# One DMA transpose per 256-token unit for the queries and one for the keys, with other step orders

## The chip, the cores and the metric

The kernel runs on one core of one Trainium2 chip. The metric is device time in microseconds of one execution, as a median over runs. The kernel before took 244.47 us (two runs, 244.05 and 244.89).

## The reference

Retention with a decay per head, then a feed-forward layer with a SoLU activation and a layer norm. Batch 8, 8 heads, 576 positions, head width 64; 4608 tokens, model width 512, hidden width 1024.

```python
scores = scale * np.matmul(q, k.transpose(0, 1, 3, 2))
gamma = 1.0 - 2.0 ** (-5.0 - np.arange(H))
Dmat = np.where(rel >= 0, gamma[:, None, None] ** rel[None, :, :], 0.0)   # rel = row - column
x = np.matmul(scores * Dmat[None], v)          # then tokens x 512
h = x @ w_in
e = np.exp(h - h_max); sm = e / (np.sum(e, axis=-1, keepdims=True) + 1e-09)
solu = h * sm
ln = (solu - mu) / np.sqrt(var + 1e-06) * g_ln
out = ln @ w_out
```

## The kernel before

The 4608 tokens are cut into 36 chunks of up to 128 tokens. For two batch entries at a time there are nine: four **units** of 256 tokens (two chunks each, numbered 0-1, 2-3, 4-5, 6-7) and a ninth chunk, 8, that holds the last 64 positions of both entries. Chunks 9 to 17 are the next nine, and so on to 35. A unit is loaded with one DMA of 512 KB for each of q, k and v; the ninth chunk with two of 128 KB each.

The work is a list of small steps, written out by hand as text: START, then LOOP twice (chunk numbers moved by 9 and 18), then END (numbers counted back from 35). A token such as `cq:10:v` is step `cq` for chunk 10 on VectorE (`a` ScalarE, `v` VectorE, `g` GpSimd). Each engine executes its own instructions strictly in the order of this list, and so does SyncE (SP), which issues nearly all DMAs: an instruction that waits holds everything behind it on its engine.

The steps, with their lines in the kernel before:

- `ld` (L204, L206) loads q, k or v; `lo` (L699) a quarter of w_out; `li` (L694, on GpSimd's queue) a quarter of w_in. The loads of q, k, v and w_out share 14 buffers, which go round.
- `cq`, `cv` (L228) scale q and v and cast them to 16 bits, `ck` (L194) casts k. Before, each chunk has its own buffer (q16: 5 of them, k16: 6).
- The scores need q and k transposed, in a tile qkT for each unit (3 buffers). For chunks 0 to 5 and every ninth chunk TensorE does it (`tr`, L251) and `er` (L194) copies the result out of PSUM. For all others a DMA transpose from SBUF to SBUF does it: `kd` (L259) for the keys, `kq` (L266) for the queries, one for each chunk, 52 in all. In START, `kq` and `kd` of chunks 0 to 5 do nothing.
- `sc` (L293, L299) scores, `mk` (L312) masks them, `kv` (L327) is k times v for the running state, `ad`, `d3`, `dk` (L342, L344, L368, L356) carry the state on, `av` (L385) and `fs` (L406) make the chunk's output, `ex` (L194) copies it to xT.
- `m1` (L443) is the first feed-forward matmul (eight of 128x512), `mx` (L453) its row maximum, `xp` (L459) the exponential, `so` (L468) the product, `ce` (L479, L484) a centring that only chunks 0 to 4 have, `sq` and `rt` (L494, L496, L508 to L518) the norm, `tu` (L526) and `eu` (L194) a transposition, `m2` (L541) the second matmul, `st` (L549, L554) the scaling and the store.
- `wo` (L706) casts an eighth of w_out, `mm`, `mc`, `ws` (L723, L194, L732) make its centred copy. The first five `m2` need all eight `wo`.
- `wu` (L671) issues so many matmuls of zeros whose result nothing reads: 33 in all, in START.
- The last chunk's feed-forward part is cut in halves: `hm`, `hx`, `hp`, `ho`, `ht`, `he`, `hq`, `h2`, `hw` (L564 to L664).

BANKS gives, in the order of the list, the PSUM bank (0 to 3) of each small PSUM tile.

START of before begins as below; `v` of the first unit comes after four loads of q, three of k and one quarter of w_out.

```
ld:0:k c1:0 wu:0:7 ld:0:q wu:0:1 ld:2:q ld:2:k ld:4:q ck:0:g cq:3:g ck:3:a cq:1:v ck:1:g
cq:5:v kq:2 cq:2:g cq:0:g lo:1 li:2 ld:4:k tr:1 ck:2:a tr:3 ld:0:v ...
```

Of the kernel before, what the change touches and what calls it, by code (L numbers as in the profile page):

```python
# [31 lines left out]
fs:2 cq:7:g ex:2:a ad:3 d3:3 mx:0 lo:2 cq:6:g fs:3 mk:5 sc:4 lo:0 xp:0 so:0 ck:6:g ex:3:a
ld:13:q mx:1 xp:1 mk:4 wo:4:a cv:6:g dk:3 kv:4 wo:5:a m1:3 ad:4 kd:6 wo:0:a kq:7 av:4 kq:6
cv:8:g so:1 ce:0 fs:4 ck:7:g mx:3 dk:4 m1:2 fs:5 sq:0 ce:1 kd:7 xp:3 d3:4 mx:2 ex:4:a ex:5:a
lo:3 ad:5 xp:2 cq:14:g cq:13:g wu:0:9 so:3 cv:7:g sc:6 sc:7 ld:9:k m1:4 mk:7 kv:6 mk:6 tu:1
wo:1:a ld:8:q ad:6 wo:6:a rt:0 so:2 ld:9:v ce:3 wo:7:a d3:6 ld:8:k tu:0 dk:6 mx:4 mm:0 ck:9:g
m1:5 ce:2 ck:10:a eu:1:a ad:7 ld:9:q mc:0:a sq:1 dk:5 kd:0 eu:0:v cq:8:g av:6 fs:6 fs:7 xp:4
# [22 lines left out]
st:5 kd:11 mx:8 eu:6:a sc:10 tu:7 sq:7 rt:7 ld:18:q m2:6 kv:9 mk:10 kd:13 eu:7:a m2:7 ld:13:v  # L60
kq:14 ad:9 cv:12:g d3:9 xp:8 so:8 av:9 ad:10 dk:9 fs:10 fs:9 tu:8 sc:12 st:6 ex:9:v m1:9
ld:18:k eu:8:v mk:12 kv:11 st:7 kq:13 sc:11 ex:10:a sq:8 mx:9 ad:11 m1:10 mk:11 cq:16:g rt:8
ck:16:g xp:9 so:9 cq:18:g m2:8 dk:11 av:11 fs:12 kd:14 ld:20:k d3:11 ad:12 fs:11 tu:9 mx:10
eu:9:v ex:11:a m1:11 sc:13 cv:13:g xp:10 cq:15:g ld:15:v m2:9 kd:16 ex:12:a
# [2 lines left out]
kq:-1 sc:-3 cv:-3:g d3:-7 sq:-8 dk:-7 kv:-4 ld:0:v so:-7 ld:0:k mk:-4 m1:-5 ld:0:q st:-9 rt:-8
cq:0:g st:-8 mx:-6 xp:-6 ad:-4 d3:-4 mk:-3 kq:-2 av:-4 dk:-4 so:-6 ck:-2:a sq:-7 fs:-3 ad:-3
mx:-5 fs:-4 ex:-3:a tu:-6 ck:0:g ex:-4:a kd:-2 sc:-1 tr:0 cv:-1:g cv:-2:g tu:-7 kv:-2 d3:-5
m1:-3 eu:-6:a mk:-1 er:0:v ad:-2 xp:-5 dk:-5 so:-5 sc:-2 mk:-2 mx:-3 rt:-7 cv:0:g eu:-7:a  # L70
m1:-4 av:-2 fs:-2 sq:-5 sq:-6 tu:-5 d3:-2 dk:-2 ad:-1 xp:-3 mx:-4 eu:-5:a m2:-6 ex:-2:a rt:-6
# [41 lines left out]
def kernel(  # L113
# [111 lines left out]

    def scaled(n, key, out, table, engine):
        dst = half.tile([P, H, D], F16, name=out, bufs=5)
        engine.tensor_tensor(  # L228
            out=dst, in0=T.pop((key, n)), in1=table.unsqueeze(2).to_broadcast([P, H, D]),
            op=ALU.mult,  # L230
        )
# [4 lines left out]

    def ck(n, e="g"):
        k16 = half.tile([P, H, D], F16, name="k16", bufs=6)
        copy(ENG[e], k16, T.pop(("kf", n)))
        T["k16", n] = k16  # L240

    def cv(n, e="g"):
        scaled(n, "vf", "v16", gkt if chunks[n][1] == 4 else gk[:, 8 * half_of(n) : 8 * half_of(n) + 8], ENG[e])
# [9 lines left out]
                )  # L253
        T["tp", n] = tp

    def kd(n):
# [2 lines left out]
        nc.sync.dma_start_transpose(  # L259
            out=turned(n)[:, 1, half_of(n)], in_=T["k16", n].rearrange("p h d -> p (h d)")  # L260
        )

    def kq(n):
        if chunks[n][1] == 4 or n < BY_DMA:
            return
        nc.sync.dma_start_transpose(  # L266
            out=turned(n)[:, 0, half_of(n)], in_=T.pop(("q16", n)).rearrange("p h d -> p (h d)")
        )
# [511 lines left out]
```

## Time and profile before

| | |
|---|---|
| median of the runs | 244.47 us |
| profiled execution, its own time | 246.94 us |
| its span, first to last instruction | 245.1 us |
| mean granted TensorE clock | 0.950 |
| matmuls, transposes by TensorE included | 2721, PE busy 211.1 us (86%) |
| VectorE, ScalarE, GpSimd busy | 181.4, 158.1, 161.8 us |
| moved by DMA | 48.42 MB, mean 198 GB/s |

The groups that the steps of this case are priced with, from the profile's list of instruction groups (engine, what, count, mean duration):

| step | engine and shape | count | mean ns |
|---|---|---|---|
| m1 | PE 128x512 | 280 | 394 |
| mk | DVE 128x512 from PSUM | 72 | 683 |
| mx, so | DVE 128x1024 | 35, 35 | 1216, 1217 |
| xp | ACT 128x1024 | 35 | 1115 |
| er, eu | ACT, DVE 128x1024 | | 1012, 681 |
| cq | POOL, DVE 128x512 | 28, 8 | 1062, 731 |
| ck | POOL, ACT 128x512 | 13, 18 | 640, 621 |
| dk, d3 | POOL 128x512, 128x256 | 32, 24 | 1070, 612 |
| kd, kq | SP, issue of one DMA transpose | 26, 26 | medians 1290, 1296 |

A reader may go by the time at which `m1` of a chunk starts, which is found by counting groups of eight L443 matmuls in PE's timeline: the first starts at 33.66 us, the fourth at 43.73, that of chunk 12 at 98.40, chunk 21 at 150.90, chunk 30 at 205.85, chunk 34 at 225.93.

### The profile page before, as it was taken

The numbers are of one execution on the slowest core, as the hardware profiler recorded it, in microseconds if no ns is written. First come the engines' busy times: TensorE is split into PE (matmuls) and PEld (weight loads), VectorE is DVE, ScalarE is ACT, GpSimd is POOL, SyncE is SP. The second block draws the span as 40 slices with busy tenths as digits, with TensorE's granted clock in tenths as the row PEclk, the third lists the DMA queues.
The fourth block names the chain that finished last, engine by engine and source line by source line (L and its number), as shares of the span: only waits on it lengthen the run. The fifth ranks groups of instructions, "written<-read, shape, count | busy, mean of one in ns | idle before, by whom it ended". The sixth has DMA issues, their size and how long they took to land.

```text
span 245.1 us, 6736 instructions
## 1 busy us (share of the span) xinstructions
PE 211.1 (86%) x2721; PEld 114.1 (47%) x2721; DVE 181.4 (74%) x289; ACT 158.1 (64%) x261; POOL 161.8 (66%) x249
## 2 busy tenths in 40 slices
PE   5166499999978999998599999995699999799993
PEld 1052264556534555545345555552345544555551
DVE  0173659999779888995659897991669898799731
ACT  2013036969695376979539548967439458689891
POOL 1393698859499655898716795789617695996121
PEclk9997689999999999999679999999689999999999
DMA  7999998799989999989949999999948998101125
GB/s 188 267 303 236 298 260 146 206 224 219 233 225 233 299 162 270 199 234 235 222 123 215 244 214 214 198 260 197 270 126 201 216 198 192 24 4 43 45 87 173
DMA packets 99456, 48.42 MB, mean 198 GB/s; under 512 B 43872, under 2 KB 93408, under 8 KB 99424
## 3 DMA queue, kind: packets, MB, share of 16 engines
q1 hardware_dynamic: 97216, 46.54, 89.8%
q0 software_dynamic: 576, 1.05, 2.3%
q10 hardware_dynamic: 1632, 0.40, 0.9%
q8 instruction: 21, 0.34, 0.7%
q14 instruction: 11, 0.09, 0.2%
HBM read 32.77 MB, written 9.44 MB: 172 GB/s over the span
## 4 chain that ended last, share of the span: by engine, by line
PE 46%; DMA 18%; DVE 9%; SPq 8%; ACT 7%; POOL 6%; issue 5%; POOLq 0%; DVEq 0%; ACTq 0%
PE o L541 16%; PE h L443 14%; DMA qkT<-q 7%; DMA vf<-in_v_dram 6%; PE lp L526 4%; SPq L204 4%; DMA qf<-in_q_dram 4%; DVE u L468 3%; SPq L206 3%; PE x L385 3%; ACT xT L194 2%; PE sc L293 2%; POOL s L356 2%; ACT e L459 2%; DMA kf<-in_k_dram 2%
## 5 line engine op out<-in xcount | busy, mean ns | idle before, releaser
L443 PE MATMUL h<-w_in,xT 128*128 128x512 f16 x280 | 69.8, 394 | 0.6 <-DVE u L468 0.4
L541 PE MATMUL o<-w_cen,uT 128*128 128x512 f16 x240 | 56.5, 379 | 0.1
L312 DVE TENSOR_TENSOR ret<-sc,tris 128x512 f16<-128x512 f32 x72 | 46.1, 683 | 8.3 <-PE sc L299 6.7
L459 ACT ACTIVATE e<-h,nm 128x1024 f32<-128x1024 f32 x35 | 39.0, 1115 | 12.1 <-DVE nm L453 10.4
L468 DVE SCALAR_TENSOR_TENSOR u<-h,e 128x1024 f16<-128x1024 f32 x35 | 42.5, 1217 | 4.7 <-ACT e L459 4.6
L453 DVE TENSOR_REDUCE nm<-h 128x1 f32<-128x1024 f32 x35 | 42.6, 1216 | 3.6 <-PE h L443 3.6
L443 PEld LDWEIGHTS <-xT 128*128 128x128 f16 x280 | 26.2, 101 | 29.7 <-issue 3.7
L541 PEld LDWEIGHTS <-uT 128*128 128x128 f16 x280 | 25.8, 98 | 29.0 <-issue 2.4
L356 POOL TENSOR_TENSOR s<-t,small 128x512 f16<-128x512 f32 x32 | 34.2, 1070 | 6.3 <-DVE t L344 4.6
L228 POOL TENSOR_TENSOR q<-qf,small 128x512 f16<-128x512 f32 x28 | 29.7, 1062 | 12.9 <-DMA qf<-in_q_dram 9.5
L228 POOL TENSOR_TENSOR v<-vf,small 128x512 f16<-128x512 f32 x29 | 32.0, 1106 | 6.6 <-DMA vf<-in_v_dram 6.5
L496 ACT ACTIVATE sq<-u,su 128x1024 bf16<-128x1024 f16 x30 | 34.5, 1151 | 1.1 <-DVE u L468 1.1
L194 ACT CAST xT<-x 128x512 f16<-128x512 f32 x27 | 19.1, 723 | 22.7 <-PE x L385 15.3
L549 ACT ACTIVATE o_sb<-o,rs 128x512 f32<-128x512 f32 x35 | 23.9, 690 | 14.2 <-issue 7.5
L514 POOL TENSOR_SCALAR w<-ss,w 128x1 f32<-128x1 f32 x31 | 8.2, 265 | 32.1 <-ACT sq L496 30.3
L526 PE MATMUL lp<-ident,u 128*128 128x128 f16 x280 | 22.7, 229 | 7.3 <-DVE t L344 7.0
L526 PEld LDWEIGHTS <-u 128*128 128x128 f16 x280 | 18.7, 102 | 12.8 <-issue 7.6
L194 ACT COPY uT<-lp 128x1024 f16<-128x1024 f16 x17 | 17.2, 1011 | 10.7 <-PE lp L526 10.7
L228 DVE TENSOR_TENSOR q<-qf,small 128x512 f16<-128x512 f32 x8 | 5.9, 731 | 22.4 <-DMA qf<-in_q_dram 12.0
L518 POOL TENSOR_TENSOR rs<-w,mhalf 128x1 f32<-128x1 f32 x36 | 19.8, 549 | 3.0
L293 PE MATMUL sc<-qkT 64*64 64x128 f16 x512 | 14.6, 226 | 7.7 <-DVE ret L312 6.0
L368 POOL TENSOR_TENSOR s<-t,small 128x256 f32<-128x256 f32 x24 | 14.7, 612 | 6.4 <-DVE t L344 4.1
(71 smaller groups left out, 252.3 us busy)
## 6 DMA issues: line engine op xcount, KB each, us to landing
kf<-in_k_dram SPq DMA_DIRECT2D x16, 512.0 KB, 5.8
qf<-in_q_dram SPq DMA_DIRECT2D x16, 512.0 KB, 6.7
vf<-in_v_dram SPq DMA_DIRECT2D x16, 512.0 KB, 6.7
out_dram<-o_sb SPq DMA_DIRECT2D x32, 256.0 KB, 4.7
w_out<-in_moe_w_out_dram SPq DMA_DIRECT2D x4, 512.0 KB, 6.8
w_in<-in_moe_w_in_dram POOLq DMA_DIRECT2D x4, 256.0 KB, 7.2
vf<-in_v_dram SPq DMA_DIRECT2D x8, 128.0 KB, 5.5
qf<-in_q_dram SPq DMA_DIRECT2D x8, 128.0 KB, 4.8
```

The costliest lines, as they stand in the source:

```text
L194: (engine.copy if engine is nc.scalar else engine.tensor_copy)(out=out, in_=in_)
L228: engine.tensor_tensor(out=dst, in0=T.pop((key, n)), in1=table.unsqueeze(2).to_broadcast([P, H, D]), op=ALU.mult,)
L312: nc.vector.tensor_tensor(out=r, in0=s, in1=m, op=ALU.mult)
L356: nc.gpsimd.tensor_tensor(out=s16, in0=t.unsqueeze(2).to_broadcast([P, 4, 2, D]), in1=gd.unsqueeze(3).to_broadcast([P, 4, 2, D]), op=ALU.mult,
L443: nc.tensor.matmul(out=h[:, i * 512 : (i + 1) * 512], lhsT=xT[:, d], rhs=w_in16[:, d, i * 512 : (i + 1) * 512], start=d == 0, stop=d == 3,)
L453: nc.vector.tensor_reduce(out=nm, in_=T["h", n], axis=AX.X, op=ALU.max, negate=True)
L459: nc.scalar.activation(out=e, in_=T["h", n], func=ACT.Exp, bias=T.pop(("nm", n)), accum_out=s)
L468: nc.vector.scalar_tensor_tensor(out=u, in0=T.pop(("h", n)), scalar=-1.0, in1=T.pop(("e", n)), op0=ALU.mult, op1=ALU.mult, accum_out=su,)
L496: nc.scalar.activation(out=s, in_=T.pop(("v", n)), func=ACT.Square, scale=-float(DFF), bias=T.pop(("su", n)), accum_out=ss,)
L526: nc.tensor.transpose(out=lp[:, c], in_=u[:, c * P : (c + 1) * P], identity=ident)
L541: nc.tensor.matmul(out=o, lhsT=uT[:, c], rhs=w[:, c], start=c == 0, stop=c == NF - 1)
L549: nc.scalar.activation(out=o_sb, in_=T.pop(("o", n)), func=ACT.Copy, scale=T.pop(("rs", n)))
```

## The change

A unit's two chunks share one 16-bit buffer for q (3 buffers of a unit) and one for k (4), in place of one buffer for each chunk. One DMA transpose of 128 x 1024 turns a unit's queries and one its keys; 26 DMA transposes in place of 52. Chunks 0 to 5 and the ninth chunks still go through TensorE.

```diff
+    def cast(key, n):
+        if key == "v16":
+            return half.tile([P, H, D], F16, name=key, bufs=5)
+        u = unit(n)
+        if (key, "pair", u) not in T:
+            T[key, "pair", u] = half.tile(
+                [P, 2, H, D], F16, name=key, bufs=3 if key == "q16" else 4
+            )
+        return T[key, "pair", u][:, half_of(n)]
...
-    def kd(n):
+    def turn(n, i, key):
         if chunks[n][1] == 4 or n < BY_DMA:
             return
+        assert (key, n) in T and (key, n + 1) in T
         nc.sync.dma_start_transpose(
-            out=turned(n)[:, 1, half_of(n)], in_=T["k16", n].rearrange("p h d -> p (h d)")
+            out=turned(n)[:, i].rearrange("p t a b -> p (t a) b"),
+            in_=T[key, "pair", unit(n)].rearrange("p t h d -> p (t h d)"),
         )
```

LOOP is the same list but for `kq` and `kd`: sixteen tokens become eight, each right behind the second of the two casts that it reads (`ck:6:a kd:6`, `cq:10:v kq:9`, `ck:10:v kd:9`, `cq:11:v kq:11`, and so on).

START and END are other lists, and BANKS another string. No `wu` is left. The front of START and the back of END:

```diff
-ld:0:k c1:0 wu:0:7 ld:0:q wu:0:1 ld:2:q ld:2:k ld:4:q ck:0:g cq:3:g ck:3:a cq:1:v ck:1:g
...
+c1:0 ld:0:k ld:0:q ld:0:v li:0 li:1 li:2 li:3 c2:0 cq:0:g ld:2:k ld:2:q ld:4:q lo:0 lo:1 lo:2
+lo:3 ld:2:v ck:0:a tr:0 er:0:a ck:3:a cq:1:v kq:0 cq:4:g ld:4:k ck:1:v tr:1 er:1:v kd:0 cq:3:g
+tr:3 er:3:v cq:2:v kq:2 cv:0:g ld:6:k ck:2:v tr:2 er:2:a kd:2 ld:6:q cv:1:g sc:0 ck:4:g tr:4
+er:4:a cq:5:g kq:4 ck:5:a tr:5 er:5:v kd:4 cv:2:v mk:0 sc:1 ld:9:q kv:0 mk:1 ld:4:v ad:0
+cv:3:g d3:0 av:0 ad:1 dk:0 fs:1 fs:0 sc:3 ex:0:v m1:0 ld:9:k mk:3 kv:2 sc:2 ex:1:a mx:0 ad:2
+m1:1 mk:2 cq:7:g ck:7:g xp:0 so:0 ce:0 cq:9:g dk:2 av:2 fs:3 ld:11:k d3:2 ad:3 fs:2 tu:0 mx:1
+eu:0:v ex:2:a m1:2 sc:4 cv:4:g xp:1 cq:6:g kq:6 ld:6:v wo:0:a wo:1:v wo:2:g wo:3:a wo:4:v
+wo:5:g wo:6:a wo:7:v m2:0 ex:3:a ld:11:q d3:1 cv:5:g ck:6:a kd:6 so:1 ce:1 sq:0 tu:1 ld:13:q
+rt:0 mk:4 sc:5 mx:2 eu:1:a m1:3 ...
...
-eu:-4:a hp:0:0 m2:-3 ht:0:1 he:0:1:v m2:-4 ho:0:0 sq:-2 hc:0 rt:-3 st:-3 tu:-2 ht:0:0 rt:-4
-mx:-1 eu:-2:a m2:-7 xp:-1 m2:-5 st:-4 he:0:0:a so:-1 tu:-1 rt:-2 hq:0:0:a st:-7 hq:0:1:a
-eu:-1:v rt:0 m2:-2 h2:0:0 sq:-1 st:-5 st:-2 hw:0:0:v rt:-1 m2:-1 st:-1 h2:0:1 hw:0:1:v
+eu:-4:a sq:-3 dk:-1 m1:-1 cv:0:g sc:0 m2:-4 mx:-2 eu:-3:v mk:0 xp:-2 st:-4 mx:-1 xp:-1 so:-2
+sq:-2 av:0 rt:-3 fs:0 ex:0:v rt:-2 m2:-3 tu:-2 so:-1 st:-3 eu:-2:a tu:-1 sq:-1 rt:-1 m2:-2
+eu:-1:a m2:-1 st:-2 st:-1 hm:0:0 hx:0:0 hm:0:1 hx:0:1 hp:0:0 hp:0:1 ho:0:0 ho:0:1 hc:0 ht:0:0
+he:0:0:v ht:0:1 he:0:1:a hq:0:0:a hq:0:1:a h2:0:0 rt:0 h2:0:1 hw:0:0:a hw:0:1:v
```

SP's first loads are therefore, after: k, q, v of unit 0-1; k, q of unit 2-3; q of 4-5; four quarters of w_out; v of 2-3; k of 4-5; k, q of 6-7.

More of the change, by code (lines that the diff above doesn't have):

```diff
@@ L32 @@
[L32 to L37, printed above, removed]
@@ new lines @@
+wo:5:g wo:6:a wo:7:v m2:0 ex:3:a ld:11:q d3:1 cv:5:g ck:6:a kd:6 so:1 ce:1 sq:0 tu:1 ld:13:q
+rt:0 mk:4 sc:5 mx:2 eu:1:a m1:3 mk:5 kv:4 av:4 st:0 dk:1 ad:4 fs:4 d3:3 ld:8:q xp:2 so:2 ce:2
+m2:1 cv:6:g ld:8:k tu:2 ld:11:v dk:4 mx:3 d3:4 sq:1 ex:4:a ck:9:a ld:9:v fs:5 ck:12:a m1:4
+ad:5 cq:10:v kq:9 sc:6 xp:3 eu:2:v rt:1 ld:8:v st:1 cv:7:g sq:2 so:3 ce:3 mk:6 mx:4 m2:2 tu:3
+ex:5:a eu:3:v sc:7 cq:13:g xp:4 rt:2 mk:7 m1:5 dk:3 cq:8:g ld:13:k ck:10:v kd:9 st:2 kv:6 av:6
+fs:6 ad:6 dk:5 m2:3 mx:5 sq:3 ck:8:a d3:6 so:4 ce:4 ex:6:a dk:6 xp:5 rt:3 cq:12:g cq:11:v
@@ new lines @@
+kq:11 fs:7 tr:8 m1:6 ad:7 so:5 cv:9:g sq:4 er:8:a rt:4 tu:4 tu:5 ex:7:a st:3 ld:15:k ck:11:v
+kd:11 eu:4:a sq:5 dk:7 m1:7 cv:8:g sc:8 mm:0 mc:0:a ws:0:v ws:1:v ws:2:g ws:3:v ws:4:v ws:5:g
+ws:6:v ws:7:v m2:4 mx:6 eu:5:v mk:8 xp:6 st:4 mx:7 xp:7 so:6 sq:6 ld:15:q av:8 cv:10:g sc:9
+rt:5 fs:8 ex:8:v rt:6 ck:13:g cq:14:g kq:13 ck:14:a kd:13 m2:5 tu:6 m1:8 cv:11:v so:7 mk:9
+st:5 mx:8 eu:6:a sc:10 tu:7 sq:7 rt:7 ld:18:q m2:6 kv:9 mk:10 eu:7:a m2:7 ld:13:v ad:9 cv:12:g
+d3:9 xp:8 so:8 av:9 ad:10 dk:9 fs:10 fs:9 tu:8 sc:12 st:6 ex:9:v m1:9 ld:18:k eu:8:v mk:12
@@ L49 @@
+kv:11 st:7 sc:11 ex:10:a sq:8 mx:9 ad:11 m1:10 mk:11 cq:16:g rt:8 ck:16:g xp:9 so:9 cq:18:g
+m2:8 dk:11 av:11 fs:12 ld:20:k d3:11 ad:12 fs:11 tu:9 mx:10 eu:9:v ex:11:a m1:11 sc:13 cv:13:g
+xp:10 cq:15:g kq:15 ld:15:v m2:9 ex:12:a
 """
 LOOP = """
-ld:11:q d3:1 cv:5:g ck:6:a so:1 kq:7 kd:6 kq:6 sq:0 tu:1 ld:13:q rt:0 mk:4 sc:5 mx:2 st:-1
-eu:1:a kv:-55 m1:3 mk:5 kv:4 av:4 st:0 dk:1 ad:4 fs:4 d3:3 ld:8:q xp:2 so:2 m2:1 cv:6:g ld:8:k
-tu:2 ld:11:v dk:4 mx:3 d3:4 sq:1 ex:4:a ck:9:a ld:9:v fs:5 ck:12:a m1:4 ad:5 cq:10:v sc:6 kd:9
@@ L60 @@
[L60 to L64, printed above, removed]
+ld:11:q d3:1 cv:5:g ck:6:a kd:6 so:1 sq:0 tu:1 ld:13:q rt:0 mk:4 sc:5 mx:2 st:-1 eu:1:a kv:-55
@@ new lines @@
+m1:3 mk:5 kv:4 av:4 st:0 dk:1 ad:4 fs:4 d3:3 ld:8:q xp:2 so:2 m2:1 cv:6:g ld:8:k tu:2 ld:11:v
+dk:4 mx:3 d3:4 sq:1 ex:4:a ck:9:a ld:9:v fs:5 ck:12:a m1:4 ad:5 cq:10:v kq:9 sc:6 xp:3 eu:2:v
+rt:1 ld:8:v st:1 cv:7:g sq:2 so:3 mk:6 mx:4 m2:2 tu:3 ex:5:a eu:3:v sc:7 cq:13:g xp:4 rt:2
+mk:7 m1:5 dk:3 cq:8:g ld:13:k ck:10:v kd:9 st:2 kv:6 av:6 fs:6 ad:6 dk:5 m2:3 mx:5 sq:3 ck:8:a
+d3:6 so:4 ex:6:a dk:6 xp:5 rt:3 cq:12:g cq:11:v kq:11 fs:7 tr:8 m1:6 ad:7 so:5 cv:9:g sq:4
+er:8:a rt:4 tu:4 tu:5 ex:7:a st:3 ld:15:k ck:11:v kd:11 eu:4:a sq:5 dk:7 m1:7 cv:8:g sc:8 m2:4
@@ new lines @@
+mx:6 eu:5:v mk:8 xp:6 st:4 mx:7 xp:7 so:6 sq:6 ld:15:q av:8 cv:10:g sc:9 rt:5 fs:8 ex:8:v rt:6
+ck:13:g cq:14:g kq:13 ck:14:a kd:13 m2:5 tu:6 m1:8 cv:11:v so:7 mk:9 st:5 mx:8 eu:6:a sc:10
+tu:7 sq:7 rt:7 ld:18:q m2:6 kv:9 mk:10 eu:7:a m2:7 ld:13:v ad:9 cv:12:g d3:9 xp:8 so:8 av:9
+ad:10 dk:9 fs:10 fs:9 tu:8 sc:12 st:6 ex:9:v m1:9 ld:18:k eu:8:v mk:12 kv:11 st:7 sc:11
+ex:10:a sq:8 mx:9 ad:11 m1:10 mk:11 cq:16:g rt:8 ck:16:g xp:9 so:9 cq:18:g m2:8 dk:11 av:11
+fs:12 ld:20:k d3:11 ad:12 fs:11 tu:9 mx:10 eu:9:v ex:11:a m1:11 sc:13 cv:13:g xp:10 cq:15:g
@@ L65 @@
+kq:15 ld:15:v m2:9 ex:12:a
 """
 END = """
[L67 to L71, printed above, removed]
@@ L72 @@
-fs:-1 xp:-4 dk:-1 dk:-3 so:-3 sc:0 mk:0 so:-4 m1:-2 av:0 sq:-3 fs:0 st:-6 ex:0:a ex:-1:v sq:-4
-tu:-3 tu:-4 mx:-2 hm:0:0 rt:-5 hm:0:1 eu:-3:v hx:0:0 xp:-2 hx:0:1 so:-2 hp:0:1 m1:-1 ho:0:1
-eu:-4:a hp:0:0 m2:-3 ht:0:1 he:0:1:v m2:-4 ho:0:0 sq:-2 hc:0 rt:-3 st:-3 tu:-2 ht:0:0 rt:-4
-mx:-1 eu:-2:a m2:-7 xp:-1 m2:-5 st:-4 he:0:0:a so:-1 tu:-1 rt:-2 hq:0:0:a st:-7 hq:0:1:a
-eu:-1:v rt:0 m2:-2 h2:0:0 sq:-1 st:-5 st:-2 hw:0:0:v rt:-1 m2:-1 st:-1 h2:0:1 hw:0:1:v
+d3:-7 cv:-3:g ck:-2:a kd:-2 so:-7 sq:-8 tu:-7 rt:-8 mk:-4 sc:-3 mx:-6 st:-9 eu:-7:a m1:-5
@@ new lines @@
+mk:-3 kv:-4 av:-4 st:-8 dk:-7 ad:-4 fs:-4 d3:-5 ld:0:q xp:-6 so:-6 m2:-7 cv:-2:g ld:0:k tu:-6
+dk:-4 mx:-5 d3:-4 sq:-7 ex:-4:a fs:-3 m1:-4 ad:-3 sc:-2 xp:-5 eu:-6:v rt:-7 ld:0:v st:-7
+cv:-1:g sq:-6 so:-5 mk:-2 mx:-4 m2:-6 tu:-5 ex:-3:a eu:-5:v sc:-1 xp:-4 rt:-6 mk:-1 m1:-3
+dk:-5 cq:0:g st:-6 kv:-2 av:-2 fs:-2 ad:-2 dk:-3 m2:-5 mx:-3 sq:-5 ck:0:a d3:-2 so:-4 ex:-2:a
+dk:-2 xp:-3 rt:-5 fs:-1 tr:0 m1:-2 ad:-1 so:-3 sq:-4 er:0:a rt:-4 tu:-4 tu:-3 ex:-1:a st:-5
+eu:-4:a sq:-3 dk:-1 m1:-1 cv:0:g sc:0 m2:-4 mx:-2 eu:-3:v mk:0 xp:-2 st:-4 mx:-1 xp:-1 so:-2
@@ L77 @@
+sq:-2 av:0 rt:-3 fs:0 ex:0:v rt:-2 m2:-3 tu:-2 so:-1 st:-3 eu:-2:a tu:-1 sq:-1 rt:-1 m2:-2
+eu:-1:a m2:-1 st:-2 st:-1 hm:0:0 hx:0:0 hm:0:1 hx:0:1 hp:0:0 hp:0:1 ho:0:0 ho:0:1 hc:0 ht:0:0
+he:0:0:v ht:0:1 he:0:1:a hq:0:0:a hq:0:1:a h2:0:0 rt:0 h2:0:1 hw:0:0:a hw:0:1:v
 """
 BANKS = """
-012301321032103032102013123031031203103212103202130230123023021320321302132012003210320301301230
-212013213201232013201323021320312031203103202302120312303201301320313201320131230132103210321021
-323120313201231023013020101230120231203102
+012301232301230123012012310230123021203123120322013220132013201321032103210213231230321031213201
@@ L83 @@
+201321132013201320132012301230123120102103012302120132132012201320132013201321032103210213231230
+32103121320120132101321032103210321
 """
@@ L224, in turned @@
         return T["qkT", u]
+    def cast(key, n):
[7 more added lines that the diff above has]
+        return T[key, "pair", u][:, half_of(n)]
     def scaled(n, key, out, table, engine):
-        dst = half.tile([P, H, D], F16, name=out, bufs=5)
+        dst = cast(out, n)
         engine.tensor_tensor(
@@ L237, in ck @@
     def ck(n, e="g"):
-        k16 = half.tile([P, H, D], F16, name="k16", bufs=6)
+        k16 = cast("k16", n)
         copy(ENG[e], k16, T.pop(("kf", n)))
@@ L254, in tq, with kd @@
         T["tp", n] = tp
-    def kd(n):
+    def turn(n, i, key):
         if chunks[n][1] == 4 or n < BY_DMA:
             return
+        assert (key, n) in T and (key, n + 1) in T
         nc.sync.dma_start_transpose(
-            out=turned(n)[:, 1, half_of(n)], in_=T["k16", n].rearrange("p h d -> p (h d)")
+            out=turned(n)[:, i].rearrange("p t a b -> p (t a) b"),
+            in_=T[key, "pair", unit(n)].rearrange("p t h d -> p (t h d)"),
         )
     def kq(n):
[L264 to L268, printed above, removed]
+        turn(n, 0, "q16")
+    def kd(n):
+        turn(n, 1, "k16")
     def tr(n):
```

22 lines of the change are left out of this document (removed).

## The prediction, made before the changed kernel ran

> **What bounds the kernel now.** First the page's forty slices and its chain of waits.
>
> ```profile
> PE   5166499999978999998599999995699999799993
> PEclk9997689999999999999679999999689999999999
> DMA  7999998799989999989949999999948998101125
> PE 46%; DMA 18%; DVE 9%; SPq 8%; ACT 7%; POOL 6%; issue 5%; POOLq 0%; DVEq 0%; ACTq 0%
> ```
>
> PE has three weak places: the first 34 us, one hole in each pass through LOOP, the last slices. Elsewhere it is the bound, with VectorE close behind. So I went to the table by stage.
>
> ```profile
> core 0: us, PE busy (x) PEld busy (x) DVE busy (x) ACT busy (x) POOL busy (x), PEclk, DMA share, GB/s
> 0.00:16.00 16.00, 7.55 (x40) 4.20 (x40) 2.92 (x7) 2.42 (x3) 6.63 (x14) 1.00 1.00 250
> 16.00:34.00 18.00, 10.70 (x221) 6.52 (x222) 10.53 (x18) 3.12 (x5) 11.41 (x14) 0.72 1.18 256
> 121.30:175.80 54.50, 49.07 (x658) 25.99 (x656) 42.14 (x66) 37.90 (x63) 37.94 (x59) 0.94 1.13 214
> ```
>
> For 34 us the DMA engines are full and the others wait for data; one pass (nine chunks) takes 54.5 us of which PE is busy 49.1. The hole inside a pass, in the timelines of DVE, PE and SP:
>
> ```profile
> 118.08 0.69 DVE L228 TENSOR_TENSOR q<-qf,small 128x512 f16<-128x512 f32 x1 [4.19 <-DMA qkT<-q]
> ...
> 119.16 2.18 PE L526 MATMUL lp<-ident,u 128*128 128x128 f16 x16 [3.21 <-DVE t L344]
> 121.13 3.62 PE L443 MATMUL h<-w_in,xT 128*128 128x512 f16 x8
> ...
> 108.35 2.64 SPq L259 DMA_TRANSPOSE qkT<-k  x1
> 111.04 1.29 SPq L206 DMA_DIRECT2D vf<-in_v_dram  x2
> 112.44 0.57 SPq L554 DMA_DIRECT2D out_dram<-o_sb  x1
> 113.11 3.37 SPq L266 DMA_TRANSPOSE qkT<-q  x2
> ```
>
> The cast cq:20 needs a q16 buffer that the transpose issued at 113.11 still reads; VectorE stands 4.19 us, PE 3.21, and PE's next eight matmuls take 3.62 us in place of 1.89 because its clock has fallen. SP has no pause from 92 to 122 us: it is late, not blocked.
>
> **Part 1, the transposes in LOOP: -7 us.** The issue of one (512 packets) takes SP 1.19 us at the least, 84.2 us for all 52 in its timeline. A 128x1024 one is not in the trace. Bounds: 1.2 us if the issue is a fixed cost, 2 x 1.3 = 2.6 by packets; I take 2.4, twice the least, since a plain load shows packets to count for something (0.46 us at the least). Data: twice as much, some 0.8 us longer. What helps is the order. Between 92.4 and 113.1 SP issues five transposes before kq:18 (1.93, 1.91, 1.95, 1.22, 2.64 = 9.65 us); after, one stands there (2.4), so kq:18 can go 7.2 us earlier, at 105.9, behind its cast cq:19 (done 104.4). It lands 4.84 + 1.2 + 0.8 = 6.8 us on, at 112.7, and VectorE comes to cq:20 at 113.9. The wait is gone with 1.2 us to spare; next late is VectorE itself (42 to 46 us of work a pass). I count the 3.2 us of PE and little of the slow clock, 3.5 a pass, -7 for two. If that cover fails, 0 or a loss: each merged transpose waits on SP for the second cast, with loads and stores queued behind it, and lands about 2 us later after its issue: +2 a pass. Ends: -10 and +4.
>
> [...]
>
> **Part 2, the front of START: +12.7 us.** PE is in order, and now tr:4 stands before sc:1, kv:0, av:0 and m1:0, so all of them wait for k of unit 4-5, SP's twelfth load. Ahead of and with it: 12 x 0.524 MB, w_in 1.05, the tables 0.26: 7.6 MB. The GB/s row moves 7.92 MB in its first five slices (6.13 us each: 188, 267, 303, 236, 298), so 7.6 MB at about 29.6 us. From there a chain of one engine after the other: ck 0.64, tr 0.45, er 1.01 on ACT, ck:5 0.62, tr 0.45, er 0.68, cv 0.71, mk:0 and mk:1 2.74, ad 0.42, d3 0.61, dk 1.04, fs 0.39, sc 0.35 = 10.1. So m1:0 starts at 39.7 (33.66 before). Then VectorE is the bound up to the fourth m1, behind mk:3 1.37, mx 1.22, ad 0.42, mk:2 1.37, so and ce 2.13, ad 0.42, mx 1.22, eu 0.68, three wo, so and ce 2.13, mk:4 1.37. No row has wo on VectorE; the centring of the same shape is 0.42 in 16 bits, a 128x256 scaling from PSUM 0.484; between 0.4 and 1.0 I take 0.70, the q cast's size. Sum 14.4, and sc 0.35: fourth m1 at 54.5, where it was 43.73: +10.8. In this stretch the list before has `wu`, which keeps PE at work; without them, PE's clock is likely halved around m1:0 as it was after the gap at 116 to 119: one m1 on the chain, 3.62 - 1.89 = +1.7, and I add nothing for the second, which VectorE covers; +0.2 for hand-overs. From the fourth m1 to chunk 12 the list holds the same work; before it took 54.7 us, like a pass, and I leave it so. SP meanwhile stands at kq:6 until GpSimd has cast q of chunks 6 and 7 (after d3:2, some 46.5 us), with the load of v for 6-7 behind it. Its consumer cv:6 comes ten or more us later, so I cost it at nothing; uncovered it would be +5. Ends: +6 (k lands at 27, VectorE's order less strict) and +18.
>
> [...]
>
> **Part 3, END: +8 us.** Before, the last chunk's halves run among the last chunks' steps. After, hm stands behind m2 of chunk 34 and nothing covers it. From the end of m1:34, before: 227.82 to 245.1, 17.3 us. After: sc and mk of the last chunk ahead of mx 1.9, mx 1.22, xp 1.31, ex 0.73, so 1.30, sq (ahead of eu on ACT) 1.35, eu 1.01, m2 1.74 = 10.6, tu being covered by sq; then hm 1.74, hx 0.84, two hp 1.8, ho 0.76, ht 0.4, he 0.59, two hq 1.9, a sum 0.38, rt 1.08, hw 0.48, and 3.3 from hw to the end as now: 13.3. Together 23.9, +6.6. From m1 of chunk 30 to that of 34 the list is LOOP's, where five such steps took 21.5 without the hole, against 20.1: +1.4. Ends +4 and +9. A stall in front of m2:34 would be hidden no longer.
>
> The sum on the profiled execution: 245.1 + 12.7 - 7 + 8 = 258.8 us of span; 1.84 us lie around it (246.94), and the median of 244.47 is 2.47 below that. So 244.47 + 13.7 = 258.2.
>
> **Rivals.**
>
> SP is the pacemaker, and the two ends are given back (0.18). For it: SP without a pause, 84 us in transposes; one kq lands in time for 4.19 us of VectorE. If the merged issue is a fixed 1.3 us, SP gets about 50 us free. A pass falls to PE's own work, 48.4 us in the stage table for the pass from 66.9, -6 each; the nine chunks in front likewise, -6. Then 244.5 + 12.7 - 12 - 6 + 8 = 247.2: not slower. It decides if transposes take under 1.5 us each on SP. If k of 4-5 also came by 22 us (w_in's transfers giving way) it would be 239.6, and 236 with END at its low end. Against: the DMA engines are at 9 tenths anyway, and their backlog stretches issues.
>
> The merged transposes hold SP (0.20). Each waits for two casts, up to 4.9 us where SP waited for a k cast before, and all loads and stores are in order behind. Loop +4 in place of -7: 269.2. For it: one q and one k transpose on time is all the present slack (1.2 us above). Against: SP runs late, so most casts are done when it gets there.
>
> That nothing merges is excluded: the changed program has 26 transposes of 128x1024.
>
> **How the numbers follow.** My forecast has 0.62, by itself 250 to 267. Slower by over 2% is above 249.4, faster below 239.6; 2% is about what a measurement of this kernel can tell. Of the first rival 0.06 lies below 239.6, 0.10 within 2% and 0.02 above; of the forecast 0.02 lies within. Slower 0.60 + 0.20 + 0.02 = 0.82; same 0.12; faster 0.06. Range 248 to 270: it leaves out half of the first rival, the second's upper half and the tails.
>
> **What would show it.** The first L443 matmul near 39.7 us, released through L251 by the k load; the fourth group near 54.5; chunk 12's near 109; no wait of L228 on DVE for a transpose in LOOP; passes near 50; from the last full m1 to the end some 24 us with PE mostly idle. SP's transposes at 2.4 us. Wrong: k of 4-5 landing well before 27, a first m1 before 36, or passes of 54 and more.

## The result, and the profile after

| | before | after |
|---|---|---|
| median | 244.47 us | 263.85 us (262.96 to 264.74) |
| ratio, 95% interval | | 1.079 [1.062, 1.097] |
| profiled execution, own time | 246.94 us | 264.74 us |
| its span | 245.1 us | 263.0 us |

The changed kernel is slower by 19 us; 258.2 was predicted, 248 to 270. Ratios, here and below, leave out executions over 1.5% slower than the fastest of the same kernel; one trace below, that of the spread `ws`, is of such an execution. The starts of `m1` cut the 17.9 us between the two spans into stages (fourth m1: the fourth in order of time; END's last 24 us hold the halved chunk):

| stage | before | after | difference | predicted |
|---|---|---|---|---|
| start to m1 of chunk 0 | 33.65 | 39.52 | +5.87 | +6.0 |
| to the fourth m1 | 10.06 | 16.40 | +6.34 | +6.7 with the slow clock |
| to chunk 12 | 54.68 | 61.36 | +6.68 | 0 |
| to chunk 21 (first pass) | 52.49 | 48.31 | -4.18 | -3.5 |
| to chunk 30 (second pass) | 54.96 | 52.95 | -2.01 | -3.5 |
| to chunk 34 | 20.08 | 18.10 | -1.98 | +1.4 |
| end of the last m1 to the end | 17.29 | 24.46 | +7.17 | +6.6 |

The forty slices and the chain of waits, after:

```profile
PE   0024359779988299999979999989599999999861
PEclk9999999979999869999999999999899999999977
DMA  7999990499958049979999998999977649512211
PE 43%; DVE 21%; DMA 11%; SPq 7%; issue 6%; POOL 5%; ACT 5%; POOLq 0%; DVEq 0%
```

PE does nothing in the first two slices and little in the two behind. The DMA engines, which before fell below 4 tenths in the last slices alone, now stand empty twice, in slice 7 (39.5 to 46 us) and in slice 14 (85.5 to 92): what the loads wait for is itself late. VectorE's share of the chain went from 9% to 21%. The stage table of after, cut at the m1 starts:

```profile
core 0: us, PE busy (x) PEld busy (x) DVE busy (x) ACT busy (x) POOL busy (x), PEclk, DMA share, GB/s
0.00:39.50 39.50, 11.10 (x164) 7.78 (x164) 8.82 (x17) 6.42 (x8) 13.44 (x22) 1.00 1.09 273
39.50:55.90 16.40, 12.66 (x168) 6.17 (x164) 14.49 (x23) 8.47 (x15) 11.46 (x15) 0.99 0.43 89
55.90:117.30 61.40, 53.35 (x668) 27.70 (x666) 50.19 (x78) 37.63 (x63) 40.95 (x60) 0.92 0.74 175
117.30:165.60 48.30, 46.40 (x661) 24.93 (x657) 42.37 (x65) 37.90 (x63) 38.24 (x59) 1.00 1.11 239
165.60:218.50 52.90, 48.56 (x662) 25.41 (x656) 42.77 (x65) 37.88 (x63) 37.49 (x58) 0.97 0.88 189
218.50:238.50 20.00, 20.00 (x291) 11.01 (x284) 16.32 (x25) 17.66 (x29) 15.97 (x26) 1.00 0.46 124
238.50:263.00 24.50, 15.31 (x105) 7.88 (x104) 9.19 (x18) 13.52 (x26) 4.38 (x13) 0.87 0.18 58
```

The second row is VectorE's: busy 14.5 of 16.4 us. The third holds 61.4 us with PE busy 53.4; that is the stage the prediction passed over. The first pass is nearly all PE (1.9 us idle), the second has a hole left (4.3).

The front, in PE's timeline of after (start, duration, engine, line, operation, count, and in brackets the idle time ahead with its releaser):

```profile
29.78 0.61 PE L260 MATMUL tp<-ident,k 128*128 128x128 f16 x4 [2.93 <-POOL k L193]
...
39.52 2.99 PE L453 MATMUL h<-w_in,xT 128*128 128x512 f16 x8
```

The cast of k of chunks 4 and 5, which frees tr:4, ran at 29.11 us. From there m1 of chunk 0 is 10.4 us off, through the chain that the prediction walks, and it takes 2.99 us in place of 1.89.

The hole between the fourth m1 and chunk 12, in VectorE's timeline:

```profile
83.09 4.86 DVE L742 TENSOR_TENSOR w_cen<-w_out,warm 128x512 f16<-128x512 f16 x6 [4.88 <-ACT warm L193]
87.87 1.21 DVE L463 TENSOR_REDUCE nm<-h 128x1 f32<-128x1024 f32 x1
```

And in PE's:

```profile
90.33 0.26 PE L395 MATMUL x<-ret,v 128*64 128x128 f16 x1 [5.33 <-DVE ret L322]
...
92.44 3.60 PE L551 MATMUL o<-w_cen,uT 128*128 128x512 f16 x8
```

The changed START has `mm:0 mc:0:a` and all eight `ws` in a row; before, they stand in ones and twos among the steps of several chunks. VectorE reaches the first `ws` 4.88 us before ScalarE's `mc` is done, then does six of them, and only then the row maximum and the masks that PE needs: PE stands 5.33 us and afterwards runs eight matmuls in 3.60 us in place of 1.89.

The wait for a query buffer is shorter than before, but it is still there in both passes. In the first, VectorE's timeline and then PE's:

```profile
134.59 0.69 DVE L237 TENSOR_TENSOR q<-qf,small 128x512 f16<-128x512 f32 x1 [2.04 <-DMA qkT<-q]
...
136.81 0.62 PE L536 MATMUL lp<-ident,u 128*128 128x128 f16 x8 [1.38 <-DVE u L478]
137.27 1.89 PE L453 MATMUL h<-w_in,xT 128*128 128x512 f16 x8
```

VectorE stands 2.04 us, PE 1.38, and the next m1 is not slow. In the second pass of after, GpSimd's timeline first:

```profile
184.96 1.04 POOL L237 TENSOR_TENSOR q<-qf,small 128x512 f16<-128x512 f32 x1 [2.12 <-DMA qkT<-q]
```

PE's timeline there:

```profile
188.08 0.64 PE L536 MATMUL lp<-ident,u 128*128 128x128 f16 x8 [3.24 <-DVE u L478]
188.53 3.58 PE L453 MATMUL h<-w_in,xT 128*128 128x512 f16 x8
```

VectorE's own cast starts at the same moment, 184.97, after 3.02 us idle for which the profile names no releaser. It is the picture of the hole before: a cast that waits for a transpose which still reads its buffer, PE idle over 3 us, a slow m1 behind. Before, VectorE stood 4.19 and 6.20 us there and PE 3.21 and 3.82. The transposes themselves, from the list for the lines that read or write qkT (minimum, median and maximum in ns, first and last start):

```profile
L269 SPq DMA_TRANSPOSE qkT<-q x13: 1232/1262/4685, 48.1 to 213.5; - x13
L269 SPq DMA_TRANSPOSE qkT<-k x13: 1256/2099/5189, 52.8 to 215.9; - x13
```

At the least a transpose of 128x1024 keeps SP 1.23 us, one of 128x512 kept it 1.19. All 26 together take 51.9 us of SP against 84.2 for the 52.

### The profile page after: what moved, and what is told of

The parts are those of the page before. It is cut to its first block, busy times and chain, and to the rows that moved or that the text cites. A ratio compares the mean times of both kernels' runs of the same rounds, so it can differ in the third digit from the quotient of the medians.

```text
span 263.0 us, 6642 instructions
## 1 busy us (share of the span) xinstructions
PE 207.4 (79%) x2688; PEld 110.9 (42%) x2688; DVE 184.1 (70%) x290; ACT 159.5 (61%) x261; POOL 161.9 (62%) x248
## 4 chain that ended last, share of the span: by engine, by line
PE 43%; DVE 21%; DMA 11%; SPq 7%; issue 6%; POOL 5%; ACT 5%; POOLq 0%; DVEq 0%
PE h L453 15%; PE o L551 13%; SPq L203 5%; DVE u L478 5%; DVE ret L322 4%; DMA kf<-in_k_dram 4%; DMA vf<-in_v_dram 4%; PE lp L536 3%; PE sc L303 3%; DVE nm L463 3%; PE x L395 2%; DMA qf<-in_q_dram 2%; DVE w_cen L742 2%; PE x L416 2%; PE kp L337 1%
## 5 line engine op out<-in xcount | busy, mean ns | idle before, releaser
L453 PE MATMUL h<-w_in,xT 128*128 128x512 f16 x280 | 70.6, 398 | 0.2
L551 PE MATMUL o<-w_cen,uT 128*128 128x512 f16 x240 | 58.5, 388 | 0.9 <-ACT o_sb L559 0.4
L366 POOL TENSOR_TENSOR s<-t,small 128x512 f16<-128x512 f32 x32 | 33.5, 1047 | 8.3 <-DVE t L352 4.2
L237 POOL TENSOR_TENSOR v<-vf,small 128x512 f16<-128x512 f32 x32 | 34.6, 1084 | 2.5 <-DMA vf<-in_v_dram 2.5
L559 ACT ACTIVATE o_sb<-o,rs 128x512 f32<-128x512 f32 x35 | 23.9, 684 | 13.7 <-POOL s L378 3.9
L193 ACT CAST xT<-x 128x512 f16<-128x512 f32 x28 | 20.5, 733 | 17.1 <-PE x L416 9.3
L536 PE MATMUL lp<-ident,u 128*128 128x128 f16 x280 | 21.6, 221 | 8.8 <-DVE u L478 5.5
L536 PEld LDWEIGHTS <-u 128*128 128x128 f16 x280 | 17.7, 99 | 16.2 <-DVE u L478 6.2
L260 PE MATMUL tp<-ident,q 128*128 128x128 f16 x40 | 5.2, 273 | 22.2 <-POOL q L237 20.7
L193 ACT COPY qkT<-tp 128x1024 f16<-128x1024 f16 x7 | 7.0, 1000 | 22.3 <-PE tp L260 22.3
L237 DVE TENSOR_TENSOR q<-qf,small 128x512 f16<-128x512 f32 x8 | 7.9, 985 | 15.4 <-DMA qf<-in_q_dram 10.3
```

Of the source, the lines that this page charges most:

```text
L237: engine.tensor_tensor(out=dst, in0=T.pop((key, n)), in1=table.unsqueeze(2).to_broadcast([P, H, D]), op=ALU.mult,)
L366: nc.gpsimd.tensor_tensor(out=s16, in0=t.unsqueeze(2).to_broadcast([P, 4, 2, D]), in1=gd.unsqueeze(3).to_broadcast([P, 4, 2, D]), op=ALU.mult,
L453: nc.tensor.matmul(out=h[:, i * 512 : (i + 1) * 512], lhsT=xT[:, d], rhs=w_in16[:, d, i * 512 : (i + 1) * 512], start=d == 0, stop=d == 3,)
L536: nc.tensor.transpose(out=lp[:, c], in_=u[:, c * P : (c + 1) * P], identity=ident)
L551: nc.tensor.matmul(out=o, lhsT=uT[:, c], rhs=w[:, c], start=c == 0, stop=c == NF - 1)
L559: nc.scalar.activation(out=o_sb, in_=T.pop(("o", n)), func=ACT.Copy, scale=T.pop(("rs", n)))
```

## The experiments

The theory: START costs 12 us in front and nearly 7 more by its block of `ws`; END 5; and LOOP wins because its casts wait less for a query buffer, not because SP issues fewer DMAs. Against it stood that the merged transposes themselves are what costs, or wins. In what follows, ratios are to the kernel before as run beside them, where it took 247.3 to 247.7 us, over 1% more than in the first table; medians in us are therefore held against each other only among these runs.

**Undo START and END, keep the merged transposes.**

```diff
 START, END: those of before, BANKS too, with kq and kd merged behind their second cast
-    bufs=3 if key == "q16" else 4
+    bufs=5 if key == "q16" else 4
```

> START, END and BANKS of the kernel before, with the merged transposes and the LOOP of after; five q buffers of a unit in place of three, since the order of before's START needs them. Theory (the merge itself shortens the two passes of LOOP, the loss is all in the new START and END): about 244.5 - 6 = 238.5 us, from m1 of chunk 12 to that of chunk 30 about 101 us in place of 107.5. Rival (the shorter passes in after come from the later, emptier start of LOOP, not from the merge): 243 to 246 us, passes as before.

241.75 us, 0.977 [0.967, 0.987]. The fourth m1 is at 43.68 again and the tail 17.7 us; the passes take 45.9 and 47.0. So the loss is in the lists, and merging, with five unit buffers, is no loss. What the shorter passes owe to merging and what to the buffers, this run does not tell. Two holes stay: keys of chunk 11 turned late (4.16 us), and 5.59 us in END, where GpSimd stands at a q load.

**Undo only the merging: two DMAs from the unit buffer, one behind the other.**

```diff
-        nc.sync.dma_start_transpose(out=turned(n)[:, i]..., in_=T[key, "pair", unit(n)]...)
+        for t in range(2):
+            nc.sync.dma_start_transpose(out=turned(n)[:, i, t], in_=T[key, "pair", unit(n)][:, t]...)
```

> The kernel after, in which each merged transpose is issued as two of 128x512 at the same place; buffers and all orders as in after. Theory (the number of DMAs counts: SP takes 1.23 us at the least for one of either size, so eight more cost it some 10 us a pass): the passes of LOOP go back to 53 or 54 us each, total 267 to 270. Rival (the place of the transposes in the order and the larger buffers made the gain, not their number): within 1 us of after, 263 to 265.

268.23 us, 1.084 [1.073, 1.095], against 1.079 [1.062, 1.097] with one DMA; passes of 50.4 and 52.9 against 48.3 and 52.9. But three other runs below with the LOOP and the buffers of the changed kernel (END of before, w_out later, warming) took 47.2 to 50.9 and 51.2 to 53.9 us for them. With order and buffers held, half the DMAs are worth nothing here that trace or ratio can tell from the scatter.

**Undo only END.**

```diff
 END: that of before, with kq and kd merged, and BANKS to fit; START and LOOP as changed
```

> The kernel after with the END of before (its transposes merged, the keys' one right behind their cast). Theory (the last chunk's halves stand uncovered at the end of after): 5 to 7 us faster than after, 257 to 259, and from the end of the last full m1 to the end some 17 us in place of 24.5. Rival (END is bound by engine work and its order gives little): 262 to 264.

1.077 [1.069, 1.085], as the changed kernel: the 5 to 7 us that the theory promised did not come. The tail does fall to 17.5 us, as predicted for the cover that before had. But chunk 30 to 34 takes 27.1 us in place of 18.1:

```profile
226.64 1.03 PE L416 MATMUL x<-qkT,s 128*128 128x128 f16 x8 [6.33 <-POOL s L366]
```

In GpSimd's timeline of the same run the reason stands ahead of the step that PE waits for:

```profile
223.97 1.04 POOL L237 TENSOR_TENSOR q<-qf,small 128x512 f16<-128x512 f32 x1 [7.54 <-DMA qf<-in_q_dram]
224.97 0.61 POOL L378 TENSOR_TENSOR s<-t,small 128x256 f32<-128x256 f32 x1
```

The cast of the last chunk's queries waits 7.54 us for their load, and the state steps queue behind it. The list of before suits loads that have arrived by then.

**Move the four w_out loads behind k of chunks 4 and 5, and k and q of 6 and 7.**

```diff
-lo:0 lo:1 lo:2 lo:3 ld:2:v ... ld:4:k ... ld:6:k ... ld:6:q cv:1:g
+ld:2:v ... ld:4:k ... ld:6:k ... ld:6:q lo:0 lo:1 lo:2 lo:3 cv:1:g
```

> The kernel after with its four loads of w_out moved behind the loads of chunks 4 to 7. Theory (m1 of chunk 0 waits for k of unit 4-5, the twelfth load): k comes some 5.4 us earlier, first m1 at 34 to 35 us in place of 39.5, total 258 to 260. Rival (VectorE's own queue, not the load, is what sets the fourth m1): first m1 earlier but the fourth still near 54 to 56, total 262 to 264.

1.055 [1.046, 1.065]. m1 of chunk 0 came at 36.88, 2.6 us earlier, where the theory had 34 to 35. GpSimd cast k at 24.18, 4.9 us earlier, right behind two v casts (22.20 to 24.18); that its row of casts sets the pace from there is read from the timeline, not tried. Thus the late k is a cause, but not the only one; the stages behind the fourth m1 did not change.

**Five unit buffers for the queries.**

```diff
-    bufs=3 if key == "q16" else 4
+    bufs=5 if key == "q16" else 4
```

> The kernel after with five q buffers of a unit in place of three, nothing else. Theory (what is left of the hole in each pass is the q cast's wait for a buffer that a transpose still reads: 2 us of VectorE in the first pass, 3.2 us of PE and a slow clock behind it in the second): no such wait, passes of 46 to 48 and 47 to 49 us in place of 48.3 and 52.9, total 4 to 7 us under after. Rival (the buffers do not matter, the passes in the first experiment were short because its START had run late): passes within 1 us of after, total within 1 us.

1.047 [1.039, 1.055]: the passes take 46.9 and 46.9. No cast waits for a transpose any more. This one number is worth 7 us in the two passes, and it is what the wait in LOOP hangs on.

**The kernel before with more buffers, nothing merged.**

```diff
-        dst = half.tile([P, H, D], F16, name=out, bufs=5)
+        dst = half.tile([P, H, D], F16, name=out, bufs=10 if out == "q16" else 5)
-        k16 = half.tile([P, H, D], F16, name="k16", bufs=6)
+        k16 = half.tile([P, H, D], F16, name="k16", bufs=8)
```

> The kernel before, transposes one per 128 tokens and all orders as they are, with ten q buffers of a chunk in place of five and eight k buffers in place of six. Theory B (the buffers alone make the passes short): passes of 47 to 49 us in place of 52.5 and 55.0, total 233 to 237 where before is 245. Theory M (merging and its places in the order are needed too, since SP issues the transposes too late): passes no shorter than 51, total 239 to 245.

238.95 us, 0.968 [0.962, 0.974]; passes of 46.8 and 48.4 against 52.5 and 55.0. The hole of before closes without any merging.

**Spread the eight ws.**

```diff
-mm:0 mc:0:a ws:0:v ws:1:v ws:2:g ws:3:v ws:4:v ws:5:g ws:6:v ws:7:v m2:4 ... mx:7 xp:7 so:6 ... ex:8:v
+mm:0 mc:0:a m2:4 ... mx:7 ws:2:g ws:0:v xp:7 so:6 ws:1:v ws:5:g ... ex:8:v ws:3:v ws:4:v ws:6:v ws:7:v
```

> The kernel after with its eight ws steps (the centred copy of w_out) spread over the steps behind the row maxima and products of chunks 6 and 7, in place of all eight behind mc. Theory (VectorE is in order and stands 4.9 us for the mean and 4.9 us in the ws, so that PE is starved for 5.3 us before av of chunk 8): the gap goes, from the fourth m1 to chunk 12's 55 to 57 us in place of 61.4, total 4 to 6 us under after. Rival (the gap only moves to m2 of chunk 5, which needs all eight): total within 2 us of after.

1.037 [1.027, 1.048]. The fourth m1 to chunk 12 takes 54.3 us in place of 61.4, so the block of `ws` is the whole of the +6.7. The run with all three mends, below, shows the stage at 52.7.

**The merged START and END of the first experiment with its two holes mended.**

```diff
 START: kd:11 moved up from behind sc:9 to behind its cast, ck:11
 END: cq:0 (chunk 35) moved down to ck:0, behind the loads
```

> The first experiment (before's START and END, merged transposes, LOOP of after, five q buffers) with two tokens moved: the keys' transpose of chunks 11 and 12 right behind its second cast, and the last chunk's q cast down to its k cast. Theory (the 4.2 us that PE stood for that transpose and the 5.6 us for the last q's load are all that kept the first experiment from the sum): 5 to 9 us under the first experiment, ratio to before 0.94 to 0.96. Rival (other waits take their place): under 3 us gained.

235.27 us, 0.955 [0.947, 0.963]: the lowest median of the study, 6.5 us under the first experiment. What is left is one wait over 3 us in END, in PE's timeline:

```profile
196.32 0.64 PE L303 MATMUL sc<-qkT 64*64 64x128 f16 x16 [4.27 <-DMA qkT<-k]
```

**The same with the keys of chunk 33 turned earlier.**

```diff
-sq:-8 dk:-7 ... so:-6 ck:-2:a kd:-2 sq:-7
+sq:-8 ck:-2:a kd:-2 dk:-7 ... so:-6 sq:-7
```

> e1_before_merged with its two END stalls mended, and in END the cast of the keys of chunk 33 and their merged transpose put ahead, right behind the eighth-last sq, so that two output stores no longer stand before it on SP. In the version with END mended as before (span 233.3), that transpose was issued at 191.6 and PE stood 4.27 us before sc of chunk 34. Theory (in this kernel a transpose costs by when it is issued, since all that follows stands on its landing): that hole goes, PE's gaps over 3 us behind chunk 12 are gone, and the time falls 3 to 5 us, to about 231 (0.93 to 0.945 of before). Rival (VectorE, at 42 to 46 us of work per nine chunks, is what sets the pace in END too, and the hole only moves): under 1.5 us, 0.95 or above.

236.58 us, 0.957 [0.952, 0.963]: no gain, so the theory fell. The hole moved two steps on:

```profile
197.19 0.61 PE L260 MATMUL tp<-ident,q 128*128 128x128 f16 x4 [4.97 <-POOL q L237]
```

It is now the q of the last chunk, whose load SP issued at 190.28 in place of 188.15, because the transpose stood ahead of it. The rival's price was right; its reason (VectorE) is not what PE waits for here. Nor is SP overworked: in its timeline it stands 7.85 us shortly before that load.

```profile
173.47 1.35 SPq L564 DMA_DIRECT2D out_dram<-o_sb  x2
182.67 1.79 SPq L269 DMA_TRANSPOSE qkT<-q  x1
```

That transpose (`kq` of chunks 33 and 34) waits for its second cast, which GpSimd starts at 181.60, and the loads of the last chunk are queued behind it. The preceding run has the same stand (175.09 to 182.93). No run moved this `kq` or the cast that it waits for.

**The unmerged counterpart: more buffers, and the same mends in END.**

```diff
 START, LOOP, buffers: as in "more buffers"
 END: kq of chunk 33 moved up behind kq of chunk 34, cq of chunk 35 down to its ck
```

> One transpose per 128 tokens throughout, the START of before, ten q and eight k buffers (e6_before_more_buffers), and in END the q cast of the last chunk moved down behind its load and kq of chunk 33 moved ahead, so that GpSimd no longer stands at a load with dk of chunk 31 behind it. It is what the merged version has to be held against. Theory (the halved number of DMAs is worth little; the buffers and the places in the order are what pays): 4 to 6 us under e6, about 234, and within 2 us of the merged version that runs beside it. Rival (26 transposes fewer on SP are worth something of their own): the merged version is faster by 5 us or more.

239.92 us, 0.969 [0.963, 0.974], no better than without the mends: here too the hole went to the last chunk's q (3.42 us). SP has no stand like that of the merged kernel here; it issues that load at 193.61, behind eight transposes from 175.89 on. Beside the merged kernel that ran with it, it is 3.3 us slower by the medians, between what the two theories gave, and the two intervals lie end to end (up to 0.9630, from 0.9634). The earlier pair, 235.27 us (which has only the q cast of the two mends in END) and 238.95 (neither), differs by 3.7. In the trace it lies in the three stages from the fourth m1 to chunk 30: 148.4 us against 144.7. So with as many bytes of buffers on both sides, merging, together with the places that its tokens have in the order, is worth some 3 to 4 us, a little over 1%. What of it is the number of DMAs and what the places was not separated with these buffers.

**All three mends of START and buffers in the changed kernel.**

```diff
 w_out loads later, ws spread, five unit buffers for q, each as above; END as changed
```

> The changed kernel with three mends of its own at once: the four transfers of w_out behind the k load of chunks 4 and 5, the eight ws steps spread over two chunks in place of in a row, and five unit buffers for the queries in place of three. END stays as changed. Theory (the terms of the ledger are separate and add): 263.9 less 2.4 to 5, less 7, less 8 to 9, so 245 to 248, 0.99 to 1.01 of before; what is left above the best merged version is the front (m1 of chunk 0 at 37, fourth m1 at 53) and the tail of 24 us. Rival (one stall moves into the next, so the terms do not add): 252 or more.

249.16 us, 1.009 [1.005, 1.013], span 245.7 against 263.0: the three terms add, the time a little above the 245 to 248 expected, the ratio within. Three rows of its stage table:

```profile
53.80:106.50 52.70, 49.60 (x673) 26.10 (x664) 48.04 (x78) 37.63 (x64) 41.59 (x61) 1.00 0.94 203
106.50:153.40 46.90, 46.36 (x665) 24.97 (x657) 42.71 (x65) 37.71 (x63) 38.03 (x59) 1.00 1.06 246
153.40:200.80 47.40, 46.55 (x662) 25.07 (x656) 42.16 (x65) 37.70 (x63) 37.60 (x58) 1.00 1.02 211
```

Its row for the `ws` on VectorE, from the list of groups (busy us, mean ns, idle before):

```profile
L742 DVE TENSOR_TENSOR w_cen<-w_out,warm 128x512 f16<-128x512 f16 x6 | 2.4, 446 | 0.0
```

PE is busy for all but under 1 us of each pass, and the clock stays at 1.00. The six `ws` on VectorE take 2.4 us, where the block took 4.86 and waited as long again. What still lies above the kernel of 235.27 us is for the most part the front (the fourth m1 at 53.8 in place of 43.9, of 12.4 us between the spans).

**Warming matmuls ahead of tr:4.**

```diff
-sc:0 ck:4:g tr:4
+sc:0 ck:4:g wu:0:9 tr:4
```

> The changed kernel with nine of the removed warming matmuls put back on PE, between sc of chunk 3 and the first transposition of chunk 4, where PE stands waiting for k of chunks 4 and 5; nothing of the result depends on them. Theory (PE's clock has fallen there: m1 of chunk 0 took 2.99 us in place of 1.89): m1 of chunk 0 in 1.9 to 2.4 us, and fourth m1 and the whole 0.5 to 1.5 us earlier. Rival (VectorE has the longer work from m1 of chunk 0 to the fourth m1 and covers it, as the prediction has it for the second): m1 of chunk 0 shorter, fourth m1 within 0.3 us, and the whole the same within its interval.

265.68 us, 1.074 [1.068, 1.080]; the fourth m1 at 55.99 against 55.93. Neither expectation holds in full, since m1 of chunk 0 is not shorter:

```profile
26.68 3.01 PE L681 MATMUL w<-warm 128*128 128x512 f16 x9
29.74 0.38 PE L260 MATMUL tp<-ident,q 128*128 128x128 f16 x4
...
36.42 1.06 PE L395 MATMUL x<-ret,v 64*64 64x128 f16 x30 [0.28 <-DVE ret L322]
38.45 0.61 PE L416 MATMUL x<-qkT,s 128*128 128x128 f16 x4 [0.97 <-POOL s L366]
39.56 3.17 PE L453 MATMUL h<-w_in,xT 128*128 128x512 f16 x8
```

The four transpositions behind the nine take 0.38 us, where they took 0.61 without them: PE runs faster. But six microseconds later, after waits of 0.3 to 1 us between short pieces, thirty small matmuls take 1.06 us, as without the nine, then four of the transpositions' size 0.61, and m1 is slow with them, 3.17 us. What the nine had brought in 3.01 us was lost while PE worked in pieces, with no wait over 1 us. (The durations alone speak here: in the changed kernel the granted clock reads 1.00 all through from 26 to 40 us, although its durations are the slow ones.) What work all through the stretch would give was not tried.

## Why the prediction came out as it did

**Bounds and direction: right.** The loss is where it was put, in START's front and in the tail, and LOOP gives part of it back.

**Front of START (+12.7 predicted, +12.2 measured): right in its steps.** k of chunks 4 and 5 was put at 29.6 us, its cast ran at 29.11; m1 of chunk 0 at 39.7, measured 39.52; the fourth at 56.4 with the slow clock, measured 55.93. The slow m1 cost 1.1 us, not 1.7. SP's stand at `kq:6`, costed at nothing, was long (from 34.4 to 48.08 us, and the DMA row is at 0 and 4 tenths from 39.5 to 52.6 for it), and yet with the `ws` spread the next stage took 54.3 us, and 52.7 with all three mends, against 54.7 before. Undoing START, in the first experiment, took the fourth m1 back to 43.68.

**"From the fourth m1 to chunk 12 the list holds the same work; before it took 54.7 us, like a pass, and I leave it so": the term that was mis-sized.** It measured 61.4. The work is the same, but its order is not: eight `ws` in a row behind a wait for `mc`. Spreading them gave 7.1 us back. The sum would have been 265.5 of span with it, against 263.0. The list had been read for what it holds, not for what stands together on one engine.

**LOOP (-7 predicted, -6.2 measured): the size is near, in part by luck; two of its steps are wrong.** The cast's wait for a transpose is what was lost before: that was right, and with five unit buffers, where it is gone, each pass fell to 46.9. But "the wait is gone with 1.2 us to spare" held in neither pass: VectorE waited 2.04 us in the first and stood 3.02 in the second. Counted from m1 of chunk 12, `kq:18` was issued 9.55 us later, where the prediction's times give 7.5, and its buffer came free 7.8 us after that, not 6.8. (Three unit buffers are little more than five of a chunk, since a ninth chunk takes a whole one.) The first pass still gained 4.2 us, because PE stood 1.6 us less in all and its clock stayed at 1.00 in place of 0.93, so that the same work took 46.4 us in place of 49.0; the clock had been counted as little. In the second the clock fell again, to 0.97 on the mean, and 2.0 came. In the kernel before, ten and eight buffers alone brought 46.8 and 48.4. And the issue of a merged transpose was taken as 2.4 us; it is 1.23 at the least, against 1.19 for half the size. A plain load was no reason for 2.4 either: in the trace of before one of 512 KB took SP 0.39 us at the least, one of 128 KB 0.61. With 1.23 us in place of 2.4 the sum would have been, by the author's estimate, some 2 us lower (1.2 us of issue in each of two passes), and further off.

**END (+8 predicted, +5.2 measured).** The tail was right (23.9 predicted, 24.5). Chunk 30 to 34 was not: +1.4 predicted, -2.0 measured, because PE is busy for all 20 us there at a clock of 1.00, and LOOP's pace of 21.5 had stalls in it (from chunk 21 to 25 the kernel with all three mends takes 19.1). That the tail is the price of the order in END is shown; that the order of before would be better here is not. Run behind the changed START, it takes 46.5 us from chunk 30 to the end against 44.5, and the total is the same.

**SP as the pacemaker.** Its condition came true in part (1.23 us each at the least, but 2.0 on the mean; 32 us of SP set free, where it counted about 50) and the first pass came out at 48.3, where it gave 48.4. It did not decide: two DMAs in place of one left the passes within the scatter, where buffers moved them by 7. The time given for it, 247.2, took a gain of 6 us in the nine chunks in front of chunk 12, which lost 6.7. **Merged transposes that hold SP:** seen, but not at its price. The transpose behind the hole of the second pass was issued at 177.36, and SP had been busy with loads from 171.81 on; it was not held. But at the end of each pass SP stands at the last `kq` until GpSimd's second cast is done, from 157.64 to 161.03 and from 205.66 to 213.49 us. With five unit buffers it stands there as long (4.2 and 7.8 us), and the passes take 46.9 all the same. What the stand delays is the loads of the last chunk.

**What is given back in END.** From m1 of chunk 30 to the end the kernel before takes 39.3 us, all others here 44.2 to 46.5: with END as changed through the tail, with END of before through a hole in front of chunk 34 or 35. The fastest kernels start m1 of chunk 30 at 188.2 to 188.4 us in place of 205.84, and lose about six of those 17.5 us again. SP issues the last chunk's q load at 202.30 in the kernel before, 3.5 us ahead of that m1; in the merged kernel with the keys moved up at 190.28, 2.1 us behind it, after its stand of 7.85 us. The unmerged kernels lose as much without such a stand, so it is not the only cause. What should go ahead of what on SP there was tried once in each, without gain, and stays open.

## What to carry to other kernels

When an order written by hand changes, read it once per engine for what now stands in a row, not only for what it holds: eight steps of one kind behind one wait cost 7 us here, about what the change won in its loop. When a cast waits for a transfer that still reads its buffer, count buffers against the transfer's whole life, issue wait included, before making transfers fewer: two more buffers of a unit won some 7 us here, half the number of transposes between nothing that could be told and 4. And a gain in the middle is worth only what the loads at the end can follow.
